# The opening of an attention and MLP kernel: first keys by halves, clears first, value halves among the smalls

## The chip, the cores and the metric

The kernel runs on one core of one Trainium2 chip. The metric is the time of one execution in device microseconds; the median of several runs is compared. Engines are named as in the profile: PE is TensorE's matmul side, PEld its weight loads, DVE is VectorE, ACT is ScalarE, POOL is GpSimd, SP is SyncE, whose queue issues the loads and stores spoken of here.

## The reference

Input is one sequence of 2048 tokens with 1024 channels, all in float32. It is cut to what matters here:

```python
h  = x + A(layernorm(x), wq, wk, wv, wo, beta)
h2 = h + B(layernorm(h), w1, b1, w2, b2)

# A: 32 heads of 32 channels; the sequence in 4 segments of 512 tokens
for s in range(4):
    logits = qs @ ks.T * 32 ** -0.5 + causal_mask
    a_dot  = softmax(logits) @ vs
    a_mem  = (phi(qs) @ M) / (phi(qs) @ z + 1e-6)      # phi(t) = t + 1 where t > 0, else exp(t)
    o      = g * a_mem + (1 - g) * a_dot               # g = sigmoid(beta), per head
    M += phi(ks).T @ vs;  z += sum(phi(ks))
# out = concat(o) @ wo
# B: gelu(y @ w1 + b1) @ w2 + b2, with d_ff = 3584
```

## The kernel before, in words

The sequence is worked in two halves of 1024 tokens, each of two segments of 512. For each half come the attention, the output projection, the second layer norm and the MLP. Only the beginning of the first half is touched by the change.

Every product in the projections is split in two parts for accuracy. A tensor `w` is kept as an upper part `wh` (rounded to the matmul's type) and a lower part `wl = w - wh`; the activations likewise as `yh` and `yl`. One block of a projection is then three matmuls (`mm3`, L113 to L116): upper by upper, upper by lower, lower by upper. With 8 blocks of 128 channels, a projection of one segment is 24 matmuls of 512 columns.

`opening` (L212) prepares the first segment. SP loads four tiles `xt` of 128 tokens, then the weights of keys and queries for the first group of heads, `beta` and `b1`. For each tile, DVE takes the statistics (L121, L125), POOL computes the scale `v` and the offset `nb` in three small instructions (L128, L129, L134), which the text calls the smalls, and ACT applies them (L244; for the fourth tile DVE does it, L246). `turn` (L248) transposes a tile with eight PE instructions in two groups of four; a group goes into one bank `pt` of PSUM, taken from three banks that it shares with the projections (`ps_dense`). ACT copies it out as `yh` (L256), and DVE forms `yl` (L263, `lower`). `halves` (L223) makes the two parts of a weight: the upper one on DVE or ACT (L225), the lower one on POOL in two instructions of four blocks each (L227). The order of all this is written out by hand at the end of `opening`: inside `in_order` every instruction is chained behind the one before it on its engine. Weights of query and value close that list.

`attention` (L297) comes next. It clears the `mask` (L302, L303) and the memory `MZ` (L308) on POOL, both placed behind the opening's last POOL instruction (`quiet = behind`). Then it goes through 8 groups of 4 heads, and in each through the two segments. `dense` (L365) is the projection of one segment: keys into `kps`, queries into `qps`, values into `vps`, one step (`yield`) after each block. For the very first segment it is interleaved with `ln1` (L195), the layer norm of the second segment, at the rate of 1.1 steps of `ln1` for each step of `dense`; afterwards with the softmax part of the segment before (`heads`). `ln1` uses one single bank of PSUM (tag `av`) for its transposes (L142), so a group of four can start only when ACT's copy (L144) and DVE's split (L146) of the group before are done.

Outside of `in_order`, a scheduler orders the instructions of each engine when the kernel is built; on the chip each engine then takes its own list strictly in that order. So an instruction that waits holds up all that stands behind it on its engine. The kernel's SP queue is such a list too, DMA issues included.

Of the kernel before, what the change touches and what calls it, by code (L numbers as in the profile page):

```python
# [16 lines left out]
P = 128  # L17
# [21 lines left out]
def raw(ap):  # L39
    return ap.bitcast(F32)  # L40


def build(tc, x, wq, wk, wv, wo, beta, w1, b1, w2, b2, out):
# [87 lines left out]

    def ln_offset(pool, m, r):
        nb = pool.tile([P, 1], F32, name="nb", bufs=4)
        nc.gpsimd.tensor_scalar(nb, m, -1.0, r, op0=ALU.mult, op1=ALU.mult)  # L134
        return nb

    def ln_transpose(pool, src, xh, xl, t4, take=None):
# [54 lines left out]
        l = apool.tile([P, DC, 512], F32R, tag=f"al{n}", name=f"{what}l{n}")  # L192
        return h, l

    def ln1(half, sl, delay=0):  # L195
        xs = []
        for t in range(4):
            xt = lnp.tile([P, D], F32, tag="ln", name="xt", bufs=4)
            r0 = half * HT + (4 * sl + t) * P
            nc.sync.dma_start(xt, x[0, r0:r0 + P, :])  # L200
            xs.append(xt)
        for _ in range(delay):
            yield
# [5 lines left out]
        yield from ln_tiles(lnp, xs, yh, yl, False, act=True,  # L209
                            fold=lambda src, t4: ln_transpose(lnp, src, yh, yl, t4, take))  # L210

    def opening():  # L212

        xs = [lnp.tile([P, D], F32, tag="ln", name="xt", bufs=4) for _ in range(4)]
        for t, xt in enumerate(xs):
            nc.sync.dma_start(xt, x[0, t * P:(t + 1) * P, :])
        raws, ws = {}, {}

        def load(n, w):
            raws[n] = wp.tile([P, DC, P], F32, tag="wr", name="wr", bufs=2)  # L220
            nc.sync.dma_start(raws[n], w[:, 0:P].rearrange("(c p) n -> p c n", p=P))

        def halves(n, hi_eng):  # L223
            ws[n] = [wp.tile([P, DC, P], F32R, tag=f"w{x_}", name=f"w{x_}", bufs=3) for x_ in "hl"]
            (nc.vector.tensor_copy if hi_eng == "vector" else nc.scalar.copy)(ws[n][0], raws[n])  # L225
            for k in (slice(0, 4), slice(4, 8)):
                nc.gpsimd.tensor_tensor(ws[n][1][:, k], raws[n][:, k], raw(ws[n][0])[:, k], op=ALU.subtract)  # L227
# [12 lines left out]

        def normal(t):
            m, r = scales[t][:2]
            if t < 3:
                nc.scalar.activation(xs[t], xs[t], AF.Identity, bias=scales[t][2], scale=r)  # L244
            else:
                nc.vector.tensor_scalar(xs[t], xs[t], m, r, op0=ALU.subtract, op1=ALU.mult)  # L246

        def turn(t):  # L248
            folds[t] = []
            for c in range(2):  # L250
                pt = ps_dense("pt").rearrange("p (a b) -> p a b", a=4)
# [4 lines left out]
                nc.scalar.copy(yh[at], pt)  # L256
                folds[t].append((at, pt))
                if c == 0 and t > 0:
                    lower(t - 1, 1)

        def lower(t, c):
            at, pt = folds[t][c]
            nc.vector.tensor_tensor(yl[at], pt, raw(yh[at]), op=ALU.subtract)  # L263
# [24 lines left out]

    def load_block(pool, w, c0, wbufs, hi_eng="vector", lo_eng="gpsimd"):
# [4 lines left out]
        split(pool, wr, wh, wl, hi_eng, lo_eng)  # L294
        return wh, wl

    def attention(half, first):  # L297
        ab = tc.alloc_tile_pool(name=f"ab{half}", bufs=1, reuse_waits="tile")
        acts["ab"] = ab
        mask = ab.tile([P, 512], F32, name="mask")  # L300
        quiet = behind if first else lambda op: op
        quiet(nc.gpsimd.memset(mask, 0.0))  # L302
        nc.gpsimd.affine_select(mask[:, 384:512], mask[:, 384:512], pattern=[[-1, P]],  # L303
                                compare_op=ALU.is_ge, fill=-1e9 / SCALE, base=0, channel_multiplier=1)
        mz_flat = acts["mz"] = ab.tile([P, NG * 132 + 96], F32, name="MZ")
        MZ = mz_flat[:, :NG * 132].rearrange("p (g e) -> p g e", g=NG)
        if half == 0:
            quiet(nc.gpsimd.memset(mz_flat, 0.0))  # L308
        else:
            nc.sync.dma_start(mz_flat, mz_dram)  # L310

        def tmp(name):
            return ab.tile([P, 512], F32, tag="tmp", name=name, bufs=5)
# [51 lines left out]
        def dense(g, sl, ws, u):  # L365
            s = 2 * half + sl
            behind = acts.pop("late", iter(()))
            kps = ps_dense("kps")
            for c in project(ws["k"], sl, "kps", kps):
                if c >= 2:  # L370
                    next(behind, None)
                yield
            kh, kl = tmpr("kh"), tmpr("kl")
            nc.scalar.copy(kh, kps)
            if s < 3:
# [913 lines left out]
```

## Time and profile before

| | us |
|---|---|
| median of 3 runs | 2388.07 |
| lowest and highest of them | 2385.95, 2391.18 |
| the profiled execution | 2383.26 |
| span of the profiled execution | 2381.4 |
| mean granted PE clock in it | 0.995 of full speed |
| busy in the span: PE, PEld | 2305.1, 1905.9 |
| DVE, ACT, POOL | 1571.3, 1244.0, 1083.3 |

All times of single instructions come from the profiled execution, counted from the start of its span. A row of the timeline gives start, duration, engine, line and operation; in brackets stands how long the engine had been idle before it, and what ended that. Matmuls are pipelined, so their durations overlap: what one costs in a row of them is the distance from start to start.

### The profile page before, as it was taken

To read this page: it belongs to the slowest core of one execution; us is meant where nothing else is said; L and a number is where in the kernel's file an instruction comes from. 1 tells how busy PE (TensorE), PEld (TensorE's weight loads), DVE (VectorE), ACT (ScalarE), POOL (GpSimd) and SP (SyncE) were. 2 spreads that over 40 slices of the span, in tenths; PEclk is the share of its full clock that TensorE was granted. 3 is DMA by queue.
4 is the path that set the end of the run, shared out by engine and by line. 5 is a ranking of instruction groups with operands and counts; after the bars stand their busy time and mean duration, and the time that the engine had idled before them with its cause. 6 is when DMAs were issued, how large, how long until landed. Compare 5 with 4: busy or idle time off the path is not lost.

```text
span 2381.4 us, 35726 instructions
## 1 busy us (share of the span) xinstructions
PE 2305.1 (97%) x11873; PEld 1905.9 (80%) x11873; DVE 1571.3 (66%) x3420; ACT 1244.0 (52%) x2587; POOL 1083.3 (45%) x1045
## 2 busy tenths in 40 slices
PE   7999999999999999999999999999999999999999
PEld 5888888877777887888888877787888788888887
DVE  5777777775466555777777776456566676566653
ACT  5676676775364344677777776354334223222321
POOL 4444444444255443455555544235444464246430
PEclk9999999999999999999999999999999999999999
DMA  5333333333466554433333334456557976476762
GB/s 164 98 89 89 83 84 85 89 106 121 144 197 204 181 168 136 124 84 88 84 84 87 81 100 125 148 168 208 164 172 224 347 261 223 154 243 229 251 220 96
DMA packets 348306, 357.49 MB, mean 150 GB/s; under 512 B 26302, under 2 KB 251610, under 8 KB 348122
## 3 DMA queue, kind: packets, MB, share of 16 engines
q1 hardware_dynamic: 284954, 318.50, 44.8%
q10 hardware_dynamic: 63168, 36.71, 5.2%
q8 instruction: 94, 1.54, 0.3%
q14 instruction: 90, 0.74, 0.1%
HBM read 227.64 MB, written 77.14 MB: 128 GB/s over the span
## 4 chain that ended last, share of the span: by engine, by line
PE 72%; DVE 7%; ACT 7%; DMA 4%; POOL 3%; issue 3%; SPq 1%; ACTq 0%; DVEq 0%; POOLq 0%
PE po L1137 21%; PE bps L762 8%; PE dps L762 5%; PE ppt L525 5%; PE po L545 5%; PE pqk L493 3%; PE kps L114 2%; PE kps L116 2%; PE kps L115 2%; PE pwo L114 2%; PE pwo L115 2%; PE pwo L116 2%; PE vps L115 2%; PE vps L114 2%; PE vps L116 2%
## 5 line engine op out<-in xcount | busy, mean ns | idle before, releaser
L509 POOL TENSOR_SCALAR pr<-pr,nm,gate 128x128 f32<-128x128 f32 (+3 forms) x512 | 323.8, 643 | 409.0 <-DVE nm L506 316.3
L502 ACT ACTIVATE pr<-pr,mx 128x256 f32<-128x256 f32 (+3 forms) x512 | 287.8, 563 | 174.8 <-DVE mx L494 170.4
L494 DVE CUSTOM_DVE_ANT_0 pr<-pqk,mask 128x256 f32<-128x256 f32 (+3 forms) x512 | 243.5, 483 | 38.2 <-PE pqk L493 35.5
L532 DVE TENSOR_TENSOR ptl<-ppt,pth 128x512 fp32r<-128x512 f32 (+1 forms) x384 | 227.3, 597 | 59.2 <-ACT pth L527 56.9
L525 PE MATMUL ppt<-ident,pr 128*128 128x128 f32 x1280 | 222.7, 277 | 1.9 <-DVE ptl L532 1.7
L527 ACT CAST pth<-ppt 128x512 fp32r<-128x512 f32 (+1 forms) x384 | 194.2, 518 | 51.3 <-PE ppt L525 46.0
L1147 DVE TENSOR_TENSOR c<-c,po 128x512 f32<-128x512 f32 x160 | 105.3, 683 | 150.4 <-PE po L1137 150.3
L91 POOL TENSOR_TENSOR wl<-wr,wh 128x1024 fp32r<-128x1024 f32 x61 | 145.9, 2392 | 115.1 <-ACT wh L90 57.2
L525 PEld LDWEIGHTS ppt<-ident,pr 128*128 128x128 f32 x1280 | 164.1, 140 | 32.2 <-DVE ptl L532 3.6
L493 PE MATMUL pqk<-ks,qs 96*128 96x256 f32 (+3 forms) x512 | 163.1, 319 | 1.5 <-DVE mx L494 1.5
L545 PE MATMUL po<-ptl,vs 128*64 128x512 f32 (+3 forms) x512 | 154.3, 311 | 5.5 <-DVE ptl L532 5.2
L545 PE MATMUL po<-pth,vs 128*64 128x512 f32 (+3 forms) x512 | 155.7, 326 | 1.3 <-ACT pth L527 1.1
L1137 PE MATMUL po<-w2h,zh 128*128 128x512 f32 x378 | 120.7, 389 | 0.0
L493 PEld LDWEIGHTS pqk<-ks,qs 96*128 96x128 f32 x512 | 96.2, 188 | 26.6 <-DVE mx L494 6.5
L506 DVE RECIPROCAL nm<-mx 128x2 f32<-128x2 f32 x256 | 42.2, 165 | 112.4 <-ACT pr L502 111.9
L1007 POOL TENSOR_TENSOR w2r<-w2r 128x512 f32<-128x512 f32 x54 | 84.3, 1574 | 59.4 <-DMA w2r<-in_B_w 54.6
L114 PE MATMUL kps<-yh,wh 128*128 128x512 f32 x256 | 108.5, 424 | 0.8 <-ACT yh L144 0.8
L114 PE MATMUL vps<-yh,wh 128*128 128x512 f32 x256 | 108.8, 425 | 0.2 <-ACT omt L475 0.2
L114 PE MATMUL qps<-yh,wh 128*128 128x512 f32 x256 | 107.0, 418 | 0.0
L114 PE MATMUL pwo<-oh,wh 128*128 128x512 f32 x256 | 105.7, 415 | 0.7 <-ACT oh L90 0.7
L1137 PE MATMUL po<-w2h,hl 128*128 128x512 f32 x322 | 102.9, 389 | 1.3 <-DVE c L1147 1.3
L116 PE MATMUL pwo<-oh,wl 128*128 128x512 f32 x256 | 102.0, 399 | 0.0
(244 smaller groups left out, 6751.5 us busy)
## 6 DMA issues: line engine op xcount, KB each, us to landing
hr<-h_dram SPq DMA_DIRECT2D x112, 448.0 KB, 4.7
w2r<-in_B_w SPq DMA_DIRECT2D x122, 256.0 KB, 4.4
r<-in_B_w SPq DMA_DIRECT2D x56, 512.0 KB, 4.7
h_dram<-ht ACTq DMA_DIRECT2D x84, 256.0 KB, 3.4
ks<-kh SPq DMA_DIRECT2D x256, 64.0 KB, 2.0
qs<-qh SPq DMA_DIRECT2D x256, 64.0 KB, 2.0
wr<-in_A_wo SPq DMA_DIRECT2D x32, 512.0 KB, 4.4
wx<-in_B_w SPq DMA_DIRECT2D x56, 256.0 KB, 3.8
```

Source lines behind the costliest of these rows:

```text
L114: nc.tensor.matmul(ps, ah, bh, start=first, stop=False)
L116: acts["mm"] = nc.tensor.matmul(ps, al, bh, start=False, stop=last)
L493: nc.tensor.matmul(pqk[:, :n], u["qs"][j][:, i * P:(i + 1) * P], u["ks"][j][:, 0:n], start=True, stop=True)
L494: nc.vector.tensor_tensor_reduce(out=st["pr"][:, offs[i]:offs[i] + n], in0=pqk[:, :n], in1=mask[:, 512 - n:512], op0=ALU.add, op1=ALU.min, ...
L502: nc.scalar.activation(pi, pi, AF.Exp, bias=mx[:, i:i + 1], scale=-1.0, accum_out=mx[:, 4 + i:5 + i])
L509: nc.gpsimd.tensor_scalar(pi, pi, nm[:, 4 + k:5 + k], gate[:, 1, 4 * g + j:4 * g + j + 1], op0=ALU.mult, op1=ALU.mult)
L525: nc.tensor.transpose(ppt[:, o:o + P], pr[:, offs[i] + jk * P:offs[i] + (jk + 1) * P], ident)
L527: nc.scalar.copy(pth[:, base:base + w], ppt[:, :w])
L532: nc.vector.tensor_tensor(o, x0, x1, op=ALU.subtract)
L545: nc.tensor.matmul(po[:, P * jk:], v, st[part][:, koff[jk]:koff[jk] + w], start=(jk, part) == (0, "pth"), stop=(jk, part) == (2, "ptl"))
L762: nc.tensor.matmul(ps, x_[:, c, :], y_[:, c, :], start=first and c == 0 and n == 0, stop=last and c == 3 and n == 2, skip_group_check=True)
L1137: nc.tensor.matmul(ps, x_[:, k], y_[k], start=opens and k == 0 and i == 0, stop=closes and k == self.KP - 1 and i == 2, skip_group_check=True)
```

## The change

It has five parts.

- The first x tile is loaded in two transfers of 512 columns each.
- The clears of `mask` and `MZ` move into a new function `attention_pool`, which is called ahead of `opening` in the first half. They are then the first work on POOL, between the two instructions that make `ident` and ahead of the smalls.
- The opening's transposes take their banks from the tags `qk` and `pt`, two each, in place of the three shared ones.
- The keys of the first segment are computed inside `opening`, by halves of 256 tokens: six blocks of the first half ahead of the fourth tile's transposes, the last two behind them, then all eight of the second half. They are 48 matmuls of 256 columns in place of 24 of 512. `dense` skips its keys in that one case, and has 16 steps there; the rate of `ln1` is 1.6.
- `halves` is split into `upper` and `under`. The second lower half of the query weights, the load of the value weights and its upper part are issued from a hook in the `ln1` of the second segment (`aside`, called after each tile's smalls). The two lower halves of the value weights are placed behind the second and third tile's `nb`.

In the built program the engines' lists differ only up to the keys of the second segment (PE) and the softmax of its first heads (ACT, DVE). PE has 24 matmuls more. On SP the load of the value weights moves behind the third x tile of the second segment, and the load of the next group's query weights from ahead of the stores of `ks` to behind those of `qs`. On POOL the second segment's smalls stand one whole chain after the other, with the lower halves of the value weights behind the second and the third chain; before, both came ahead of all of them, and the first two chains were interleaved. In the softmax of the first head, DVE's four mask reductions and PE's four `pqk` matmuls come ahead of the second segment's keys instead of among them.

```diff
-        nc.gpsimd.tensor_scalar(nb, m, -1.0, r, op0=ALU.mult, op1=ALU.mult)
+        acts["nb"] = nc.gpsimd.tensor_scalar(nb, m, -1.0, r, op0=ALU.mult, op1=ALU.mult)
...
-    def ln1(half, sl, delay=0):
+    def ln1(half, sl, delay=0, aside=None):
...
     def opening():
-        for t, xt in enumerate(xs):
-            nc.sync.dma_start(xt, x[0, t * P:(t + 1) * P, :])
+        for k in (slice(0, 512), slice(512, 1024)):
+            nc.sync.dma_start(xs[0][:, k], x[0, 0:P, k])
+        for t in range(1, 4):
+            nc.sync.dma_start(xs[t], x[0, t * P:(t + 1) * P, :])
...
+        def under(n, i):
+            k = slice(4 * i, 4 * i + 4)
+            return nc.gpsimd.tensor_tensor(ws[n][1][:, k], raws[n][:, k], raw(ws[n][0])[:, k], op=ALU.subtract)
...
-                pt = ps_dense("pt").rearrange("p (a b) -> p a b", a=4)
+                pt = psum.tile([P, 512], F32, tag=("qk", "pt")[c], name="pt", bufs=2).rearrange("p (a b) -> p a b", a=4)
...
+        kps = ws["kps"] = ps_dense("kps")
+
+        def keys(i, cs):
+            n = slice(256 * i, 256 * i + 256)
+            for c in cs:
+                mm3(kps[:, n], ws["k"][0][:, c, :], ws["k"][1][:, c, :], yh[:, c, n], yl[:, c, n], c == 0, c == DC - 1)
...
-            halves("k", "vector")
+            upper("k", "vector")
+            under("k", 0)
+            under("k", 1)
             turn(1)
             lower(1, 0)
             normal(3)
             turn(2)
             lower(2, 0)
+            keys(0, range(6))
             turn(3)
             lower(3, 0)
             lower(3, 1)
-            halves("q", "scalar")
-            load("v", wv)
-            halves("v", "scalar")
+            keys(0, range(6, DC))
+            upper("q", "scalar")
+            under("q", 0)
+            keys(1, range(DC))
+
+        def rest(t):
+            if t == 0:
+                under("q", 1)
+                load("v", wv)
+                upper("v", "scalar")
+            elif t < 3:
+                tc.add_manual_dep(under("v", t - 1).ins, acts["nb"].ins.name, NOSYNC, reason="program order")
...
-    def attention(half, first):
-        ab = tc.alloc_tile_pool(name=f"ab{half}", bufs=1, reuse_waits="tile")
-        quiet = behind if first else lambda op: op
-        quiet(nc.gpsimd.memset(mask, 0.0))
+    def attention_pool(half):
+        ab = acts["ab"] = tc.alloc_tile_pool(name=f"ab{half}", bufs=1, reuse_waits="tile")
+        mask = acts["mask"] = ab.tile([P, 512], F32, name="mask")
+        nc.gpsimd.memset(mask, 0.0)
...
-            quiet(nc.gpsimd.memset(mz_flat, 0.0))
+            nc.gpsimd.memset(acts["mz"], 0.0)
...
-            kps = ps_dense("kps")
-            for c in project(ws["k"], sl, "kps", kps):
+            kps = ws.pop("kps", None)
+            if kps is None:
+                kps = ps_dense("kps")
+                for c in project(ws["k"], sl, "kps", kps):
...
-                    interleave(d, ln1(half, 1), 1.1)
+                    interleave(d, ln1(half, 1, aside=ws.pop("rest", None)), 1.6 if first else 1.1)
...
-    first = opening()
     for half in range(2):
-        rest = attention(half, None if half else first)
+        attention_pool(half)
+        first = None if half else opening()
+        rest = attention(half, first)
```

More of the change, by code (lines that the diff above doesn't have):

```diff
@@ L207, in take @@
             return psum.tile([P, 512], F32, tag="av", name=name, bufs=1)
[L209 removed]
+        yield from ln_tiles(lnp, xs, yh, yl, False, act=True, aside=aside,
                             fold=lambda src, t4: ln_transpose(lnp, src, yh, yl, t4, take))
@@ L221, in load, with upper @@
             nc.sync.dma_start(raws[n], w[:, 0:P].rearrange("(c p) n -> p c n", p=P))
-        def halves(n, hi_eng):
+        def upper(n, eng):
             ws[n] = [wp.tile([P, DC, P], F32R, tag=f"w{x_}", name=f"w{x_}", bufs=3) for x_ in "hl"]
-            (nc.vector.tensor_copy if hi_eng == "vector" else nc.scalar.copy)(ws[n][0], raws[n])
-            for k in (slice(0, 4), slice(4, 8)):
-                nc.gpsimd.tensor_tensor(ws[n][1][:, k], raws[n][:, k], raw(ws[n][0])[:, k], op=ALU.subtract)
+            (nc.vector.tensor_copy if eng == "vector" else nc.scalar.copy)(ws[n][0], raws[n])
+        def under(n, i):
+            k = slice(4 * i, 4 * i + 4)
+            return nc.gpsimd.tensor_tensor(ws[n][1][:, k], raws[n][:, k], raw(ws[n][0])[:, k], op=ALU.subtract)
         load("k", wk)
@@ L295, in load_block, with attention @@
         return wh, wl
-    def attention(half, first):
-        ab = tc.alloc_tile_pool(name=f"ab{half}", bufs=1, reuse_waits="tile")
-        acts["ab"] = ab
-        mask = ab.tile([P, 512], F32, name="mask")
-        quiet = behind if first else lambda op: op
-        quiet(nc.gpsimd.memset(mask, 0.0))
+    def attention_pool(half):
+        ab = acts["ab"] = tc.alloc_tile_pool(name=f"ab{half}", bufs=1, reuse_waits="tile")
+        mask = acts["mask"] = ab.tile([P, 512], F32, name="mask")
+        nc.gpsimd.memset(mask, 0.0)
         nc.gpsimd.affine_select(mask[:, 384:512], mask[:, 384:512], pattern=[[-1, P]],
                                 compare_op=ALU.is_ge, fill=-1e9 / SCALE, base=0, channel_multiplier=1)
-        mz_flat = acts["mz"] = ab.tile([P, NG * 132 + 96], F32, name="MZ")
-        MZ = mz_flat[:, :NG * 132].rearrange("p (g e) -> p g e", g=NG)
+        acts["mz"] = ab.tile([P, NG * 132 + 96], F32, name="MZ")
         if half == 0:
-            quiet(nc.gpsimd.memset(mz_flat, 0.0))
+            nc.gpsimd.memset(acts["mz"], 0.0)
         else:
-            nc.sync.dma_start(mz_flat, mz_dram)
+            nc.sync.dma_start(acts["mz"], mz_dram)
+    def attention(half, first):
+        ab, mask = acts["ab"], acts["mask"]
+        MZ = acts["mz"][:, :NG * 132].rearrange("p (g e) -> p g e", g=NG)
         def tmp(name):
@@ L367, in dense @@
             behind = acts.pop("late", iter(()))
-            kps = ps_dense("kps")
-            for c in project(ws["k"], sl, "kps", kps):
-                if c >= 2:
-                    next(behind, None)
-                yield
+            kps = ws.pop("kps", None)
+            if kps is None:
+                kps = ps_dense("kps")
+                for c in project(ws["k"], sl, "kps", kps):
+                    if c >= 2:
+                        next(behind, None)
+                    yield
             kh, kl = tmpr("kh"), tmpr("kl")
```

1 line of the change is left out of this document (added).

## The prediction, made before the changed kernel ran

> **What bounds the kernel now.** I read the page's busy shares first, then the windows view over the first 100 us, and last the timeline around the hole in TensorE's work (start, length, engine and line, what it does; in brackets the idle time ahead of it and what ended it). Columns of the windows view: window, length, busy time of PE, PEld, DVE, ACT and POOL, granted clock, DMA share, GB/s.
>
> ```profile
> PE 2305.1 (97%) x11873; PEld 1905.9 (80%) x11873; DVE 1571.3 (66%) x3420; ACT 1244.0 (52%) x2587; POOL 1083.3 (45%) x1045
> ```
> ```profile
> 23.50:28.45 4.95, 0.00 (x0) 0.00 (x0) 0.62 (x3) 1.29 (x2) 4.43 (x12) 0.91 0.45 134
> 28.45:34.50 6.05, 6.05 (x19) 4.99 (x20) 2.21 (x5) 4.47 (x7) 1.21 (x4) 0.51 0.20 46
> ...
> 60.00:100.00 40.00, 38.75 (x236) 32.47 (x235) 30.38 (x98) 27.41 (x71) 19.11 (x24) 1.00 0.45 122
> ```
>
> TensorE is the bound: 97% of the span, and 38.75 of 40 us right behind the opening. The opening is the exception. From 23.50 to 28.45 PE does nothing, POOL is busy 4.43 us; ACT waits for POOL's `nb` (27.16, below) and PE for ACT's normalised tile (28.45). Then PE runs 6.05 us at clock 0.51, which loses about 6.05 x 0.49 = 3.0 us. Since everything later is PE-bound in a written order, time saved before about 60 us should reach the end.
>
> ```profile
> 4.40 1.29 DVE L121 BATCH_NORM_STATS2 st<-xt 128x6 f32<-128x512 f32 x2 [3.15 <-DMA xt<-in_A_x]
> ...
> 6.03 0.19 POOL L128 TENSOR_SCALAR v<-mv 128x1 f32<-128x1 f32 x1 [4.74 <-DVE mv L125]
> ...
> 10.62 1.10 POOL L129 TENSOR_TENSOR v<-v,mhalf 128x1 f32<-128x1 f32 x1
> ...
> 11.01 0.68 DVE L225 CAST wh<-wr 128x1024 fp32r<-128x1024 f32 x1
> ...
> 14.31 0.38 SPq L221 DMA_DIRECT2D wr<-in_A_wv  x1
> ...
> 14.75 1.87 DVE L263 TENSOR_TENSOR yl<-pt,yh 128x512 fp32r<-128x512 f32 x3
> ...
> 16.80 1.29 DVE L263 TENSOR_TENSOR yl<-pt,yh 128x512 fp32r<-128x512 f32 x2 [0.17 <-ACT yh L256]
> ...
> 17.26 1.05 ACT L225 CAST wh<-wr 128x1024 fp32r<-128x1024 f32 x1
> ...
> 18.39 5.05 POOL L227 TENSOR_TENSOR wl<-wr,wh 128x512 fp32r<-128x512 f32 x4 [4.10 <-ACT wh L225]
> ...
> 22.89 0.39 PE L114 MATMUL qps<-yh,wh 128*128 128x512 f32 x1
> 23.11 0.39 PE L115 MATMUL qps<-yl,wh 128*128 128x512 f32 x1
> ...
> 23.39 0.51 POOL L302 MEMSET mask<- 128x512 f32 x1
> ...
> 26.86 0.51 POOL L134 TENSOR_SCALAR nb<-mv,v 128x1 f32<-128x1 f32 x2
> ...
> 27.16 2.37 ACT L163 ACTIVATE xt<-xt,nb,v 128x1024 f32<-128x1024 f32 x2 [6.49 <-POOL nb L134]
> ...
> 27.45 0.19 POOL L128 TENSOR_SCALAR v<-mv 128x1 f32<-128x1 f32 x1
> ...
> 28.38 0.27 POOL L134 TENSOR_SCALAR nb<-mv,v 128x1 f32<-128x1 f32 x1
> ...
> 28.45 1.11 PE L142 MATMUL pt<-ident,xt 128*128 128x128 f32 x4 [4.95 <-ACT xt L163]
> ...
> 29.66 0.27 POOL L134 TENSOR_SCALAR nb<-mv,v 128x1 f32<-128x1 f32 x1
> ...
> 30.09 0.59 ACT L374 CAST kh<-kps 128x512 fp32r<-128x512 f32 x1
> ...
> 31.53 1.26 ACT L163 ACTIVATE xt<-xt,nb,v 128x1024 f32<-128x1024 f32 x1
> ```
>
> The queue behind the hole is POOL's: the query and value halves (18.39, four in 5.05, 1.26 each), the clears (from 23.39), then the smalls, two tiles interleaved. The first offset of the second segment is ready near 27.1 (half of the 26.86 pair), the last at 29.93.
>
> **Clears first.** They move from 23.39 to POOL's start, where it waits 4.74 us for `mv`. One clear of 0.51 stands ahead of the end of `ident`, which is needed only by the first transposes, after 8.5. Cost nothing; if that cover were gone it would be 0.51.
>
> **First x tile in two transfers.** The statistics wait 3.15 us for that tile, so at best one of the two (1.29 / 2 = 0.65) starts while the second half flies; one more issue on SP pushes later tiles back by at most some 0.45 (an estimate: like the 0.38 of the 14.31 row). The second tile's chain gates the rest; I take 0, ends -0.65 and +0.45.
>
> **Keys by halves.** Before, all 24 products stand behind the last transposes. Now tokens 0 to 255 come first. The transposes now have four banks, so the third tile's no longer wait for splits, and twelve products (1.4 us) fit behind them; the fifth and sixth block need the second tile's last `yl`, the first of the three at 14.75, done near 15.4. If the clock were still low there, twelve would take twice that and end about 1 later. The price of a 256-column product is not among the keys, but the nearest row has it:
>
> ```profile
> 36.76 0.60 PE L142 MATMUL pt<-ident,xt 128*128 128x128 f32 x4
> 37.12 0.48 PE L115 MATMUL qps<-yl,wh 128*128 128x512 f32 x1
> ...
> 38.82 0.60 PE L142 MATMUL pt<-ident,xt 128*128 128x128 f32 x4
> ...
> 46.34 0.50 PE L114 MATMUL kps<-yh,wh 128*128 128x512 f32 x1 [0.56 <-ACT yh L144]
> ...
> 48.26 0.28 PE L493 MATMUL pqk<-ks,qs 96*128 96x256 f32 x1
> 48.38 0.40 PE L114 MATMUL kps<-yh,wh 128*128 128x512 f32 x1
> ...
> 53.95 0.44 PE L115 MATMUL qps<-yl,wh 128*128 128x512 f32 x1
> ...
> 57.45 0.30 PE L525 MATMUL ppt<-ident,pr 128*128 128x128 f32 x1
> 57.51 0.31 PE L358 MATMUL pmm<-vs,pkh 128*128 128x128 f32 x1
> 57.65 0.30 PE L525 MATMUL ppt<-ident,pr 128*128 128x128 f32 x1
> ...
> 59.47 0.30 PE L525 MATMUL ppt<-ident,pr 128*128 128x128 f32 x1 [0.77 <-DVE ptl L532]
> ```
>
> A 256-column product takes 0.12 to the next start (48.26 to 48.38), a 512-column one 0.22 to 0.23 (22.89 to 23.11). Ends: 0.12 and 0.23; I take 0.12, because two products with full 128x128 weights pass in 0.20 (57.45 to 57.65). So: five products left at 15.4 give 16.0; the fourth tile's eight transposes (0.36 a four, 36.76 to 37.12) end at 16.7; its copies and splits slip half a microsecond against the 16.80 row, the first `yl` ending at 16.80 + 0.65 + 0.5 = 17.95. The second half then runs 24 x 0.12 = 2.9 us, to 20.9. The queries start there instead of 22.89: **-1.9**.
>
> **POOL's order.** ACT's query cast (17.26) slips by the same 0.5 and so does the 18.39 of its halves: the two for the query run 18.9 to 21.5. A chain of smalls is 1.2 (27.45 to 28.65). Hence offsets at 22.7 and 23.9; value half, 25.2; third offset 26.4; value half, 27.7; fourth offset 28.9. The first is 4.4 us earlier, the last only 1.0. On SP the value load now stands behind the third x load of the second segment, which waits for the third tile's transposes; these precede the 14.75 splits, so it is out by 14.8 instead of 14.31. Before, load, cast and halves were through by 23.44 with POOL's two query halves in front; the cast, which now stands ahead of the first normalisation on ACT, is done well before the offset at 22.7. Cost nothing; if the load were late, each us beyond that is a us on this chain.
>
> **What is late next.** I followed each engine's new order with these durations. The first tile is normalised at 22.7 + 1.2 = 24.0 (PE: twelve query products, 2.7, to 23.7; hole 0.3). Its second group of transposes needs the one `av` bank back, which copy and split of the first group free; ACT does the key copy, exp and relu (31.53 - 30.09 = 1.4) and the second normalisation (1.2) ahead of that copy, so it starts at 26.6, and with the split (1.5 together, the rest of the 2.06 between 36.76 and 38.82 behind a group of transposes) the bank is free at 28.1. PE has nine query products after 24.4, to 26.4: hole **1.8**. On ACT the fourth normalisation, which waits for the offset at 28.9, stands ahead of the next copy: it ends at 30.2, the next transposes start at 31.6; PE has three query products, six for the values and two transposes of `pk`: hole 0.8. From there the single bank paces them by 2.06: 33.65, 35.7, 37.8, 39.8, 42.7, the last later still, because DVE's four mask reductions of the first head now come ahead of its splits and of the second segment's keys. Holes from 37 on: about 3.1 in sum. Then 23 key products bring PE to the query product of 53.95 at about 48.3, from which all engines' orders are nearly the old ones.
>
> **Sum.** From first query to that product: 53.95 - 22.89 = 31.1 before, 48.3 - 20.9 = 27.4 after: **-3.7** (4.95 idle, 3.0 clock and the 0.56 at 46.34 go; some 6 us of new holes come, about 1.4 of small gaps go too). The stall of 0.77 at 59.47 should go, its `ptl` now standing one reduction earlier with DVE ahead: **-0.8**. Total -1.9 - 3.7 - 0.8 = **-6.4**. The profiled execution took 2383.26 (span 2381.4), so 2376.9; the median of the runs shown is 2388.07, 4.8 above it, and on that scale I give **2381.7**.
>
> **The rivals.** (1) *The clock falls in a new hole.* The trace has both sides:
>
> ```profile
> 704.40 0.50 PE L762 MATMUL cps<-zh,wh 128*128 128x512 f32 x1 [2.89 <-ACT p L831]
> ...
> 1611.25 0.69 PE L762 MATMUL cps<-zh,wh 128*128 128x512 f32 x1 [2.75 <-ACT p L831]
> ```
> ```profile
> 704.40:708.00 3.60, 3.60 (x18) 2.99 (x19) 1.29 (x2) 2.75 (x5) 2.51 (x2) 1.00 0.98 293
> ...
> 1608.50:1611.25 2.75, 0.00 (x1) 0.01 (x1) 0.17 (x1) 1.71 (x2) 0.85 (x2) 1.00 0.99 290
> 1611.25:1614.72 3.47, 3.47 (x8) 2.70 (x9) 1.29 (x2) 2.62 (x5) 2.38 (x2) 0.52 0.96 289
> ```
>
> A hole of 2.75 was followed by clock 0.52, one of 2.89 kept its full clock: where the hole falls decides. My holes are at most 1.8, but between 38.3 and 42.7 PE would work about 1.9 of 4.4 us. A fall there costs about 3.0: -3.4, 2384.7. [...]
>
> (2) *Half-width keys cost like whole ones*, 0.23: 48 products, of which the second half pays 24 x 0.11 = 2.6 and the first, partly under the wait to 15.4, some 1.7: -2.1, 2386.0. For it: weight loads are as many as products, now doubled. Against: the 0.20 pair.
>
> (3) *The old hole seldom lowers the clock.* In other executions the 3.0 wasn't lost, so it can't be won: -3.4, 2384.7. At 4.95 it is longer than both holes above, so mostly it does.
>
> (4) *The other side: POOL stretched by DVE.* The power at 10.62 took 1.10 and ended with DVE's cast at 11.69; the smalls' whole chain is usually 1.2. The 10 us of POOL work from 18.9 to 28.9 are in series before the fourth normalisation. If they all doubled, the hole grows by 10: +3.6, and with a clock loss of 3.0 from it +6.6, 2394.7; it turns to a loss when they stretch by more than 64%. Against: the four halves at 18.39 took 5.05 while DVE was busy. [...]
>
> **How the numbers follow.** About 0.2% (4.8 us) is what a measurement tells from no change. Chances: forecast 0.52, (1) 0.18, (2) 0.12, (3) 0.12, (4) 0.06. Of the forecast's share nine tenths lie beyond 4.8, of (1) to (3) about a sixth: faster 0.54, same 0.40, slower 0.06. The range takes the forecast with an early first tile and medians that scatter by up to 3.1 (2388.07 to 2391.18), 2378, up to (2) with the late end of the x tiles and the same scatter, 2389.5.
>
> **What would show it.** In the new profile: clears before 6 us; first `qps` near 21; no clock row near 0.5 between 24 and 35; first L142 transposes near 24, second near 28 behind a hole of 1.8; `qps` of the second segment's L115 near 48.3; no wait for `ptl` at the second group. If the first is at 22 and `kps` starts are 0.2 apart, (2) holds; if the clock reads 0.5 near 42 to 48, (1); if value halves take over 1.6 us each, (4). A gain lost after 60 us would refute the claim that it carries.

## The result, and the profile after

The changed kernel took 2376.29 us (median of 6 runs, 2374.40 to 2382.26) against 2389.62 for the kernel before beside it: a ratio of 0.9954 (95% interval 0.9939 to 0.9968). A second comparison, with more runs, gave 2379.99 against 2387.23: 0.997 (0.9958 to 0.9981). So it is faster, by 7 to 11 us. Predicted were 2381.7 and a gain of 6.4. That fits in direction and roughly in size, but less than a third of the gain is where the prediction had put it, so that the nearness of the time is in the main luck.

The page of the changed kernel, and its windows over the opening (columns as before):

```profile
PE 2304.7 (97%) x11897; PEld 1907.4 (80%) x11897; DVE 1572.2 (66%) x3420; ACT 1243.3 (52%) x2587; POOL 1082.0 (46%) x1045
```
```profile
24.00:28.00 4.00, 3.86 (x20) 2.93 (x19) 2.16 (x6) 3.53 (x5) 3.35 (x9) 1.00 0.51 147
28.00:32.00 4.00, 2.96 (x16) 2.18 (x15) 1.88 (x6) 2.73 (x4) 2.87 (x5) 1.00 0.47 106
...
40.04:43.45 3.41, 1.81 (x13) 1.34 (x12) 1.91 (x8) 2.10 (x7) 0.00 (x0) 1.00 0.46 106
43.45:46.87 3.42, 3.42 (x13) 2.97 (x14) 2.65 (x10) 2.33 (x8) 1.29 (x3) 0.50 1.04 345
```

PE's 24 more matmuls are there. The hole at 23.5 is gone, and no clock is lowered up to 40. But PE works only 1.81 of 3.41 us from 40.04 on, and from 43.45 to 46.87 the clock is 0.50. The timeline of the changed kernel:

```profile
1.92 1.06 POOL L332 MEMSET MZ<- 128x1152 f32 x1
...
3.66 0.69 DVE L121 BATCH_NORM_STATS2 st<-xt 128x6 f32<-128x512 f32 x1 [2.40 <-DMA xt<-in_A_x]
5.07 0.69 DVE L121 BATCH_NORM_STATS2 st<-xt 128x6 f32<-128x512 f32 x1 [0.72 <-DMA xt<-in_A_x]
...
7.34 1.29 DVE L121 BATCH_NORM_STATS2 st<-xt 128x6 f32<-128x512 f32 x2 [1.33 <-DMA xt<-in_A_x]
...
16.66 0.28 PE L116 MATMUL kps<-yh,wl 128*128 128x256 f32 x1
16.78 0.28 PE L114 MATMUL kps<-yh,wh 128*128 128x256 f32 x1
...
22.71 0.40 PE L114 MATMUL qps<-yh,wh 128*128 128x512 f32 x1
...
25.67 1.30 POOL L233 TENSOR_TENSOR wl<-wr,wh 128x512 fp32r<-128x512 f32 x1
...
25.77 0.66 PE L142 MATMUL pt<-ident,xt 128*128 128x128 f32 x4
...
29.55 0.66 PE L142 MATMUL pt<-ident,xt 128*128 128x128 f32 x4 [1.04 <-DVE yl L146]
...
33.67 0.66 PE L142 MATMUL pt<-ident,xt 128*128 128x128 f32 x4 [1.16 <-DVE yl L146]
...
41.91 0.66 PE L142 MATMUL pt<-ident,xt 128*128 128x128 f32 x4 [1.22 <-DVE yl L146]
...
45.59 1.05 PE L142 MATMUL pt<-ident,xt 128*128 128x128 f32 x4
...
51.91 0.39 PE L115 MATMUL qps<-yl,wh 128*128 128x512 f32 x1
...
67.47 0.39 PE L575 MATMUL po<-pth,vs 128*64 128x384 f32 x1 [0.86 <-ACT pth L557]
...
68.38 0.39 PE L575 MATMUL po<-ptl,vs 128*64 128x384 f32 x1 [0.53 <-DVE ptl L562]
...
700.71 0.50 PE L792 MATMUL cps<-zh,wh 128*128 128x512 f32 x1 [1.50 <-ACT p L861]
...
1557.17 1.05 ACT L836 CAST wh<-wx 128x1024 fp32r<-128x1024 f32 x1 [4.42 <-DMA wx<-in_B_w]
...
1603.15 0.50 PE L792 MATMUL cps<-zh,wh 128*128 128x512 f32 x1 [1.46 <-ACT p L861]
```

The row of 51.91 is the query product that stood at 53.95 before; I call it the mark. The opening wins 2.0 us up to it and 1.9 near 100 us, as PE's matching matmuls show: the start of each one less its start before, which the texts below call the lag. The rest came later, in steps. Some steps differ from profile to profile, where the lowered clock falls otherwise. Two come in both profiles of the changed kernel, 1.3 to 1.5 us of lag each, and both show in the last rows. `cps` at 1603.15 is the matmul that waited 2.75 at 1611.25 before; now it waits 1.46. Its twin in the first half (2.89 at 704.40) now waits 1.50, at 700.71. Ahead of both stands a load of `w1` (`wx`); the row of the kernel before for the second:

```profile
1565.23 1.05 ACT L806 CAST wh<-wx 128x1024 fp32r<-128x1024 f32 x1 [5.68 <-DMA wx<-in_B_w]
```

ACT waited 5.68 us for that load, and waits 4.42 now; the whole chain behind it (casts, statistics, `nb`, normalisation, the copy of `p`) is early by the difference: from that cast to `cps` it is 46.0 us in both kernels (1565.23 to 1611.25, 1557.17 to 1603.15). Nothing in the change touches that stage. What differs there is seen in the DMA view of the stretch of that load, first before (1559 to 1566 us), then after (1552 to 1558; queue, packets, MB, share of the engines):

```profile
q1 hardware_dynamic: 2102, 1.04, 52.3%
q10 hardware_dynamic: 144, 0.26, 10.0%
q8 instruction: 1, 0.02, 0.8%
```
```profile
q1 hardware_dynamic: 2081, 1.04, 61.2%
q10 hardware_dynamic: 144, 0.26, 11.7%
```

In the kernel before, one load of 16 KB of an engine's code falls among the loads of `w1`; in the changed one it does not. Its one packet took 0.8% of 16 DMA engines' time in 7 us, some 0.9 us of one engine (an estimate); how that holds up the loads of `w1` by 1.3 us, no view here shows. The page of the kernel before counts such code loads over the span:

```profile
q8 instruction: 94, 1.54, 0.3%
```

There are 94, as many after. Counted against the records of the trace, 255.7 of TensorE's instructions start between one and the next in the mean before, 255.8 after (195 to 341 and 211 to 298 in the single; the 11873 matmuls and as many weight loads make up nearly all of them), so this is taken to be TensorE's own code, one load for some 256 instructions (an estimate from these means); the runs that add instructions to TensorE alone, below, bear it out. The change adds 47 such instructions at the start (24 matmuls and 24 weight loads, and one other less), and by that estimate every later code load stands 47 instructions earlier in the program. In the traces the code loads nearest to the two stages start at 655.5 and 1561.8 us before, at 645.4 and 1547.8 after, there ahead of the loads of `w1`. That became the theory to test.

### The profile page after: what moved, and what is told of

Same layout as the page of the kernel before. It is cut to its first block, busy times and chain, and to the rows that moved or that the text cites. A ratio compares the mean times of both kernels' runs of the same rounds, so it can differ in the third digit from the quotient of the medians.

```text
span 2373.1 us, 35777 instructions
## 1 busy us (share of the span) xinstructions
PE 2304.7 (97%) x11897; PEld 1907.4 (80%) x11897; DVE 1572.2 (66%) x3420; ACT 1243.3 (52%) x2587; POOL 1082.0 (46%) x1045
## 3 DMA queue, kind: packets, MB, share of 16 engines
q8 instruction: 94, 1.54, 0.3%
## 4 chain that ended last, share of the span: by engine, by line
PE 74%; DVE 8%; ACT 7%; DMA 4%; issue 3%; POOL 3%; SPq 0%; ACTq 0%; DVEq 0%; POOLq 0%
PE po L1167 21%; PE bps L792 8%; PE dps L792 5%; PE ppt L555 5%; PE po L575 4%; PE pqk L523 3%; PE kps L114 2%; PE kps L116 2%; PE kps L115 2%; PE vps L114 2%; PE vps L115 2%; PE vps L116 2%; PE pwo L114 2%; PE pwo L115 2%; PE pwo L116 2%
## 5 line engine op out<-in xcount | busy, mean ns | idle before, releaser
L114 PE MATMUL kps<-yh,wh 128*128 128x512 f32 (+1 forms) x264 | 110.4, 418 | 0.6 <-ACT yh L144 0.6
L115 PE MATMUL kps<-yl,wh 128*128 128x512 f32 (+1 forms) x264 | 102.8, 389 | 0.1
```

The costliest lines, as they stand in the source:

```text
L114: nc.tensor.matmul(ps, ah, bh, start=first, stop=False)
L115: nc.tensor.matmul(ps, ah, bl, start=False, stop=False)
```

## The experiments

Ratios are to the kernel before, run beside each on the same chip, with 95% intervals. The table holds what the verdicts use. "Wait for wx" is ACT's wait ahead of the cast shown above; "hole" is PE's idle time ahead of the later `cps` (from start to start it is 0.4 longer, and so it is told in the expectations).

| kernel | mark | wait for wx | hole | median | ratio |
|---|---|---|---|---|---|
| before, first profile | 53.95 | 5.68 | 2.75 | | |
| before again | 52.69 | 5.72 | 2.82 | 2388.32 | 0.9998 (0.9986-1.0011) |
| other banks | 54.28 | 5.71 | 2.78 | 2386.75 | 0.9992 (0.998-1.0003) |
| before, code moved by 256 | 53.94 | 6.12 | 3.21 | 2384.36 | 0.9994 (0.9982-1.0006) |
| before, code moved by 96 | 54.00 | 4.51 | 1.54 | 2383.06 | 0.9982 (0.997-0.9993) |
| before, code moved by 48 | 53.49 | 4.25 | 1.29 | 2378.64 | 0.9968 (0.9958-0.9978) |
| the same again | 53.61 | 4.35 | 1.40 | 2379.12 | 0.9973 (0.9961-0.9984) |
| changed, first profile | 51.91 | 4.42 | 1.46 | 2376.29 | 0.9954 (0.9939-0.9968) |
| changed again | 52.09 | 4.37 | 1.45 | 2379.99 | 0.997 (0.9958-0.9981) |
| changed, keys whole | 54.22 | 6.59 | 3.20 | 2384.54 | 0.9998 (0.9986-1.001) |
| changed, values first | 51.72 | 4.32 | 1.39 | 2380.60 | 0.9971 (0.996-0.9982) |
| changed, x tile whole | 49.04 | 4.38 | 1.44 | 2375.99 | 0.996 (0.9944-0.9976) |
| the same, code put back | 48.83 | 6.13 | 3.15 | 2379.05 | 0.9972 (0.9959-0.9985) |
| x tile whole, values first | 50.21 | 4.43 | 1.46 | 2375.09 | 0.9955 (0.9941-0.9969) |

**Both kernels once more.** No edit.

> The kernel before once more, unchanged: a second profile of it and a null comparison. Theory A (the change gains only in the opening, some 2 to 3 us; what the first pair of profiles showed beyond that, about 5 us in steps at 611, 1515 and 1611 us, was chance of which later holes meet a lowered clock): the half-clock stretches after 100 us lie at other places or are other in number than in the first profile of it (611.3, 1515.8, 1611.4, 1850.3), and this profile's span differs from 2381.4 by 3 to 10 us. Theory B (the later steps belong to the kernel and come in every execution): the half-clock stretches are at the same places within 2 us, the span within 3 us of 2381.4. Both expect a ratio to the kernel before of 1.000 within 0.002, and the hole of 4.95 us at 23.5 us with a clock near 0.5 behind it.

> The changed kernel once more, unchanged. Theory A: 2 to 3 us less than before in the opening again (the lag of TensorE's matching matmuls at 60 to 100 us is -1.8 to -3), later steps at other places than 190, 381, 704, 1520, 1611 and 1851 us; over the five rounds the ratio comes nearer to 1 than 0.9954, at 0.997 to 0.999. Theory B: the steps come at the same places, the ratio is again 0.994 to 0.997. Both expect the opening itself as in the first profile: second half of the first x tile's statistics near 5.1, first qps near 22.7, new holes of about 1.0 to 1.2 at 29.5, 33.7 and 41.9.

Theory A is right in that much of the later difference is chance: half-clock stretches of before came at other places (at about 17.9, at 28.17 and about 704.0 us, against 27.60 and 611.28 in the first profile), its mean granted clock was 0.992 in place of 0.995, and its span 2386.6 in place of 2381.4. Theory B is right in that part of it belongs to the kernel: the wait for wx and the hole are the same in both profiles of each kernel to 0.07 us, and the ratio stayed at 0.997, 7 us, where the opening shows 1.9. Neither explains the whole. The old hole did not begin at 23.5 in this profile of before, as both theories had it: PE still worked all of 23.00 to 24.00 (0.50 of it in the first profile), since the fall of the clock at 17.9 had already made the first products later (0.43 apart from 18.14 to 21.13, 0.23 behind that).

**The first x tile in one transfer**, in the changed kernel.

```diff
-        for k in (slice(0, 512), slice(512, 1024)):
-            nc.sync.dma_start(xs[0][:, k], x[0, 0:P, k])
-        for t in range(1, 4):
-            nc.sync.dma_start(xs[t], x[0, t * P:(t + 1) * P, :])
+        for t, xt in enumerate(xs):
+            nc.sync.dma_start(xt, x[0, t * P:(t + 1) * P, :])
```

> The changed kernel with the first x tile in one transfer of 1024 columns, as before; all else is as in the change. Theory C (the two transfers made the opening later, by some 1.5 us): the second tile's statistics start near 5.85 in place of 7.34, the first qps near 21.0 in place of 22.7, and TensorE's lag against before at 60 us is 1.3 to 1.8 us larger than with two transfers; the time is 1 to 2 us below the changed kernel's. Rival D (the later statistics came from the arrival of the data in that one execution, not from the split): statistics and first qps at the same times as with two transfers within 0.4 us, no difference in time.

Its timeline:

```profile
6.11 1.23 DVE L121 BATCH_NORM_STATS2 st<-xt 128x6 f32<-128x512 f32 x2
...
21.30 0.40 PE L114 MATMUL qps<-yh,wh 128*128 128x512 f32 x1
...
49.04 0.39 PE L115 MATMUL qps<-yl,wh 128*128 128x512 f32 x1
```

Theory C holds. The second tile's statistics start at 6.11 in place of 7.34, the first query product at 21.30 in place of 22.71: the split costs 1.4. Rival D falls: in all four profiles with two transfers the second tile's statistics start at 6.89 to 7.89, in six with one at 5.85 to 6.11. The mark comes 2.9 earlier, since the fall of the clock at 43.45, worth half of 3.42 us, was also missing in this profile (clock 1.00 from 20 to 60).

**Other banks of PSUM**, in the kernel before.

```diff
+    for tag in ("d", "qk", "pt"):
+        psum.tile([P, 512], F32, tag=tag, name="first", bufs=3 if tag == "d" else 2)
```

> The kernel before, with the PSUM banks of the tags qk, pt and av where the changed kernel has them (three small unused tiles are named first, so that the order of the first use is d, qk, pt, av; every engine's list is as before). In the changed kernel all 1565 PSUM tiles sit in other banks than before. Theory E (the placement in the banks, not the opening, makes the later stages shorter): the ratio to before is 0.995 to 0.998, a gain in the later stages with none in the opening. Theories A and B: 1.000 within 0.002, the same opening as before with the hole of 4.95 us.

Waits and hole are those of before, and the ratio's interval holds 1. Theory E falls: the banks don't bring the gain.

**Only the places of the code loads moved**, in the kernel before. Tiny matmuls stand ahead of all else on TensorE, which is idle there (its first work in the kernel before starts at 8.55). The tile that they write is the same in all these runs, so what it may do to the places of the other tiles is in the run with 64 too.

```diff
+    shift = psum.tile([P, 512], F32, tag="av", name="shift", bufs=1)
+    for _ in range(24):        # 12 and 64 in the other runs
+        nc.tensor.matmul(shift[0:4, 0:4], hsel, hsel, start=True, stop=True)
     first = opening()
```

> The kernel before, with 24 tiny matmuls (hsel by hsel, 4 by 4, into a tile nobody reads) ahead of everything else on TensorE, where that engine is idle until 8.55 us. They are there only to be code: TensorE's code comes in loads of 16 KB, one for every 256 of its instructions (94 of them in each run), and the 48 instructions of these matmuls move every later load of code as far ahead in the program as the change's 24 additional matmuls do. Theory F (the later gain of the change comes from that): in the runs of before, loads of code at 655.5 and 1561.8 us fall among the loads of w1 (wx, issued from 1559.1 on, landed 1565.2), in the changed kernel 6 to 7 us ahead of them in the program; so here the two holes ahead of cps (3.1 to 3.6 us between starts at 704 and 1611 in all three profiles of before, 1.84 in all three of the changed kernel) shrink to 1.8 to 1.9; the opening stays as before (nb at 27, first qps 22.6 to 24.9); the time is 2 to 6 us below before, 2382 to 2386. Rival H (the later gain comes from earlier data in the opening or from anything else in the change): both holes stay at 3.1 to 3.6, and the ratio is 1.000 within 0.0012.

> The kernel before with 12 tiny matmuls ahead of everything else on TensorE. The 24 of the first such run were 96 instructions, twice as many as meant, since each is two matmuls and two weight loads; the 12 are 48, as many as the change adds (47). Theory F: loads of code near 648 and 1554 in the program of before, ahead of the loads of w1; both holes ahead of cps at 1.8 to 1.9 us, the opening as before, the time 2382 to 2386. Rival H: holes of 3.1 to 3.6, ratio 1.000 within 0.0012.

> The kernel before with 64 tiny matmuls ahead of everything else on TensorE: 256 instructions, exactly one load of code, so that all later loads of code stand where they stand in before. A control for the tiny matmuls themselves. Theory F: both holes ahead of cps at 3.0 to 3.6 us, the load of w1 landing 5.0 to 6.0 us after its issue, the opening as before, the ratio 1.000 within 0.0012. Rival K (tiny matmuls at the start help by themselves, by warming the clock or in another way, which would also explain why the kernel with the code loads put back still was some 3 us faster than its opening's gain): the ratio is 0.997 to 0.9985 with holes of 3.0 to 3.6.

> The kernel before with 12 tiny matmuls (48 instructions) once more, beside the control with 256. Theory F: holes ahead of cps of 1.7 to 1.9, ratio again 0.996 to 0.998 (the first time 0.9968). If the first result was chance: ratio 0.998 to 1.000 with the same holes. Rival K: ratio as that of the control.

The timelines of the first run with 12 tiny matmuls, and of the one with 64:

```profile
1.31 0.74 PE L1168 MATMUL shift<-hsel 128*4 128x4 f32 x24 [1.31 <-DVE hsel L58]
...
1561.81 1.05 ACT L806 CAST wh<-wx 128x1024 fp32r<-128x1024 f32 x1 [4.25 <-DMA wx<-in_B_w]
...
1607.80 0.50 PE L762 MATMUL cps<-zh,wh 128*128 128x512 f32 x1 [1.29 <-ACT p L831]
```
```profile
1562.19 1.05 ACT L806 CAST wh<-wx 128x1024 fp32r<-128x1024 f32 x1 [6.12 <-DMA wx<-in_B_w]
...
1608.21 0.79 PE L762 MATMUL cps<-zh,wh 128*128 128x512 f32 x1 [3.21 <-ACT p L831]
```

The 12 appear as 24 matmuls, each with its weight load: 48 instructions (PE and PEld both x11897 on the page, against x11873). They do nothing for the result, the mark is at 53.5 to 53.6, between the two profiles of before, and yet the kernel before with them is about as fast as the changed kernel: 0.9968 and 0.9973. With 64, 256 instructions and so one code load by the estimate above, waits and hole return and the gain is gone: 0.9994. That the place of the code makes the gain, as theory F has it, is thereby shown, and H and K fall. With 96 instructions the hole shrinks as well, but the gain is 4.3 and not 6.4 to 7.6; whether that difference is real the intervals don't say.

Where on the way the gain arises is shown only in part. In all 14 profiles the hole goes with the place of the code: 2.75 to 3.21 us where it is moved by at most one instruction or by 255 or 256, 1.29 to 1.54 where it is moved by 47 to 96, and likewise in the first half of the sequence, 2.44 to 3.02 in five profiles of the one kind, 1.48 to 1.50 in three of the other. The DMA view shows the code load among the loads of `w1` in the kernel before and with 64 tiny matmuls, and none there in the changed kernel, in that with the whole x tile and with 12 tiny matmuls. But in the lag of both runs with 12 tiny matmuls, against the first profile of before, each of the two stages is worth 1.4 us, 2.8 together, of the 6.4 to 7.6 that their ratios come to. All later code loads move, not only these two, and the clock falls at other places; which of that gives the rest stays open.

**The parts undone.** The keys whole; then POOL's old order, once with the two transfers and once without.

```diff
-            n = slice(256 * i, 256 * i + 256)      # keys whole
+            n = slice(0, 512)
-            keys(0, range(6))
-            keys(0, range(6, DC))
...
             keys(1, range(DC))                     # values first
-
-        def rest(t):
...
-        ws["rest"] = rest
+            under("q", 1)
+            load("v", wv)
+            upper("v", "scalar")
+            under("v", 0)
+            under("v", 1)
```

> The changed kernel with its first keys whole: 24 matmuls of 512 columns behind the last transposes in place of 48 of 256 around them. Loading in two transfers, clears, banks and the order on POOL stay as in the change. Theory F: TensorE has as many instructions as before, the loads of code are back at before's places in the program, and the two holes ahead of cps are 3.1 to 3.6 us again; the opening loses what the halves gave, 1 to 2 us against the changed kernel (lag against before near 100 us: 0 to -1); the time is 2385 to 2388. Rival H: holes of 1.84 stay, and only the opening's 1 to 2 us go: 2380.5 to 2382.

> The changed kernel with POOL's order undone: all lower halves of the query and value weights ahead of the second segment's smalls again, the load and upper part of the value weights in the opening; the loading in two transfers, the clears first, the keys by halves and the banks stay. F and H both: the holes ahead of cps stay at 1.84 (TensorE's list is that of the changed kernel). The prediction's term of -3.7 for POOL's order, if it is right in size: the lag against before near 100 us, -1.7 to -1.8 in two profiles of the changed kernel, becomes 0 to +2, and the time is 2 to 4 us above the changed kernel's 2379, at 2381 to 2383. Rival J (the order on POOL is worth little, since a new hole opens for each that goes): lag near 100 us -1 to -2, no more than 1 us above the changed kernel.

> The changed kernel with the first x tile in one transfer and with POOL's old order (lower halves of query and value weights ahead of the second segment's smalls); clears first, keys by halves and banks stay. If POOL's order is worth nothing, as the run with it alone undone has it (query product of the second segment at 51.7 against 51.9 us), this one is as fast as the changed kernel with the one transfer: lag against before near 100 us of -3.5 to -5, time 2375 to 2378. If the order is worth its predicted 3.7 us once the opening is earlier: lag of -0.5 to -1.5, 2379 to 2381. Holes ahead of cps of 1.84 in both.

With whole keys, which take the 48 instructions out again, the wait for wx is 6.59, the hole 3.20, and the change brings nothing (0.9998): theory F again. The mark falls back by 2.3, from 51.91 to 54.22. This is the most that the halves are worth: the second x tile came 0.55 later in this one (statistics at 7.89 against 7.34), and products stand 0.43 apart in place of 0.23, as at half clock, up to 20.97 and again from 34.85 to 36.54, where the changed kernel has from 20 on the one stretch from 43.45 to 46.87; what the first of these cost is not shown. POOL's order is worth next to nothing: undone, the mark is at 51.72 against 51.91, as rival J had it; counted from the first query product, which came 0.6 earlier in this profile, the stretch to it is 29.6 against 29.2, so the order is worth 0.4 at most. Without the two transfers it is 50.21 against 49.04, where the one has a lowered clock from 27.4 on (0.64 from 28 to 32) and the other none (1.00 from 20 to 60). The timeline of the values first:

```profile
28.09 0.66 PE L142 MATMUL pt<-ident,xt 128*128 128x128 f32 x4 [3.05 <-ACT xt L163]
...
45.99 0.63 PE L142 MATMUL pt<-ident,xt 128*128 128x128 f32 x4
```

The first group of transposes is 2.3 later than with the change's order (28.09 against 25.77), the last only 0.4 (45.99 against 45.59): the one `av` bank paces them, and the time won at the first is waited out at the holes of 1.04 and 1.16.

**The code loads put back**, in the changed kernel with the whole x tile: 52 tiny matmuls (the loop above, into a tile of the tag `d`), 208 instructions, which with the change's 47 make nearly one code load.

> The changed kernel with the first x tile in one transfer, and 52 tiny matmuls (hsel by hsel, 4 by 4; each is two matmuls and two weight loads on the engine, so 208 instructions) ahead of everything else on TensorE, in about 3 us in which it is idle anyway. With the change's own 47 they move every later load of TensorE's code by 255 instructions against before, one whole load, and so put the loads back to the places in the program that they have in before. The opening's gain stays. Theory F: the two holes ahead of cps are 3.1 to 3.6 us again, the load of w1 that is issued near 1553 takes 5.0 us to land in place of 3.7; the lag against before near 100 us is -4.5 to -5.5, and the time is 3 to 6 us above that of the same kernel without the tiny matmuls, 2379 to 2382. Rival H (the later gain belongs to the opening's earlier work or to the other parts of the change): holes of 1.84, time 2375 to 2378.

```profile
1558.23 1.06 ACT L836 CAST wh<-wx 128x1024 fp32r<-128x1024 f32 x1 [6.13 <-DMA wx<-in_B_w]
...
1604.22 0.80 PE L792 MATMUL cps<-zh,wh 128*128 128x512 f32 x1 [3.15 <-ACT p L861]
```

Wait (6.13) and hole (3.15) come back, with the opening's gain untouched (48.83). The time is 3 above the same kernel without them, as theory F has it, though the two intervals overlap. Beside it on the same chip the kernel with the whole tile and the values first, its code loads not put back, took 2375.09, 4.0 less, although its opening ends later (50.21 against 48.83). The ratio's interval (3.6 to 9.8 us below before) holds the 5.1 us that the opening gives.

The lowest medians are those of the change without the two transfers, with either order on POOL (2375.99 and 2375.09); their ratios, 0.996 and 0.9955, are not told from the 0.9954 and 0.997 of the change as it is.

## Why the prediction was right, and where it was wrong

**Faster** was right, and the time of 2381.7 was near: the first median, 2376.29, is 1.7 below the range, the second, 2379.99, within it. The mechanism was mostly another, so that the near total is luck: most of what the opening failed to give was made up by a term that the prediction did not have. By its own steps:

- **Clears first: 0.** Right; the last is done at 2.98 (1.92 + 1.06), ahead of the first statistics.
- **x tile in two transfers: 0, ends -0.65 and +0.45.** Wrong: +1.4, three times the upper end. The first tile's statistics end nearly as before (5.07 + 0.69 = 5.76 against 4.40 + 1.29 = 5.69), but the second tile's start at 7.34 in place of 5.85. I bounded the cost by SP's issue time; it lies in the arrival of what is queued behind (DVE waits 1.33 for the second tile).
- **Keys by halves: -1.9.** Right in size, though 22.89 to 20.9 is 2.0 and not 1.9. With the whole x tile the first query product is 1.6 earlier than before (21.30 against 22.89); by the run with whole keys the halves are worth 2.3 at the mark at most. Products of 256 columns are 0.12 apart (16.66 to 16.78), so rival (2) was not it.
- **POOL's order and what is late next: -3.7.** The order of events held: first transposes 25.77 (24.0 predicted), second 29.55 (28.1), holes of 1.04, 1.16 and 1.22. With the whole x tile the stretch from first query to mark is 27.7 (21.30 to 49.04), near the predicted 27.4. But the attribution failed. The same twelve query products ahead of the transposes, which come from the rate of 1.6 and the keys' early place, already shorten the old hole from 4.95 to 3.05 with the old order on POOL; the reorder adds next to nothing.
- **Rival (1), the clock falling between 38.3 and 42.7: 0.18.** It happened in both profiles of the changed kernel, at 43.5 and 43.9, for 3.4 us at half clock: 1.7, not 3.0. PE had worked 1.81 of the 3.41 us ahead of the first of these falls.
- **Rival (3), the old hole costing less than 3.0.** True in part. The clock fell behind that hole in both profiles of the kernel before, and with 24 and 64 tiny matmuls the four transposes behind it took 1.11 and 1.12 us, as in the first profile of before, in place of 0.60: so not seldom. But the half clock lasted 6.83 us in the first profile (27.60 to 34.43) and 3.41 in the second (28.17 to 31.58), which costs half as much.
- **Rival (4), POOL stretched.** Not seen: the value half at 25.67 took 1.30, against some 1.26 before.
- **The `ptl` stall: -0.8.** It went, and came back at `po` as waits of 0.86 and 0.53 (67.47 and 68.38): about 0 in sum, as the lag is 2.0 at the mark and 1.9 near 100 us.

The opening thus gave 2.0 of the predicted 5.6 at the mark: 1.4 went to the split, up to 1.7 to rival (1), and half a microsecond to smaller slips. The rest of the gain, some 6 us by the runs that moved nothing but code (3 by the run that put it back), comes from a step that the prediction did not have. It stated that behind the mark "all engines' orders are nearly the old ones", and took the 24 more matmuls as 0.12 us each. As code they are 48 instructions, and they push code loads out from among the loads of `w1` that gate the chain to `cps`, once in each half. This accounts for some 2.8 us of it; by the runs with 12 tiny matmuls the rest goes with the place of the code too, but no trace shows at which stage.

## What to carry to other kernels

Before a difference of a few tenths of a per cent is credited to the reordering that was made, run the old kernel with the new one's number of instructions: a dozen tiny matmuls at the start gave here about what the whole change gave (0.9968 and 0.9973 against 0.9954 and 0.997), and one load's worth of them, 64, gave nothing (0.9994). A stage that waits for a load with little slack should be looked at for code loads in its DMA view. Where a single buffer paces a chain, bringing its first link forward moves the wait, not the end: here 2.3 us at the first group of transposes became 0.4 at the last.

## What the runs showed of the hardware

- Code is loaded while the kernel runs, in 94 pieces of 16 KB in the span of either kernel, and where such a piece fell among the loads of `w1`, these landed later. In the second half it did so before and with 64 tiny matmuls: median landing 5.7 and 6.1 us after the issue, ACT's wait for `wx` 5.68 and 6.12. In the changed kernel and with 12 tiny matmuls it did not: landing 4.4 and 4.2, wait 4.42 and 4.25. Over all 14 profiles the wait was 5.68 to 6.59 us in the six with the code at or near its places of before, 4.25 to 4.51 in the eight with it moved by 47 to 96 instructions. The cost fell on a load that ACT waited for.
- In the first traces of both kernels all changes of the granted clock lie on a grid of 3.41 us, and the stretches at half clock, but for one at the very end, last 3.41 or 6.83. Counted from the start of the span, the grid began at 0.29 us before and at 2.49 after, and by its fall at 28.17 at 0.86 in the second profile of before. The same hole was punished in one execution and not in the next: behind `cps` at 704.40 the clock stayed full (1.00 to 708), in the second profile of before the products behind it are 0.43 apart in place of 0.23 from 704.12 to 707.11. The mean granted clock was 0.992 in the least and 0.999 in the most of the 14 profiled executions, which over the span comes to 19 and 2 us (an estimate) and would be enough for the up to 14 us between the shortest and the longest run of one kernel.
- A stretch of that grid need not be idle for the clock to fall behind it. In the first traces of both kernels, between 24 us and the last 10 us of the span, the clock fell behind ten stretches, in which PE had worked 0.00 to 1.81 of the 3.41 us: 0.00 ahead of the fall at 27.60 before, 1.81 ahead of that at 43.45 after. Behind others it stayed full: with 1.52 (699.99 to 703.40 before) and with 1.80 and 1.83 (1507.79 to 1511.20 and 1511.20 to 1514.62 after).
